# Folding a two-dimensional Fourier stage over n as well as over m

## The chip, the cores and the metric

The kernel runs on one core of a Trainium2 chip. The core has a matrix engine (TensorE, PE in the profile; PEld are its weight loads), a vector engine (DVE), a scalar engine (ACT), a general engine (POOL) and an engine that only issues transfers and waits (SP). Each executes its own instructions in the order in which they were written; they wait for one another by semaphores. Sixteen DMA engines carry out all transfers. The metric is the device time of one execution in microseconds, the median of three runs.

## The reference

The input x is 8 batches of 3072 x 256 float32. The first part is a Fourier transform over both axes of which only the real part is kept; a router and two expert layers follow.

```python
X = np.fft.fft(x, axis=1); X = np.fft.fft(X, axis=2)
x = X.real.astype(np.float32).reshape(B * S, D)
# router: normalised rows times normalised expert embeddings, softmax, argmax
# every token goes through its own expert's relu(x @ w1[e]) @ w2[e], times its probability
h = x @ w_in
g = np.where(h > 0.0, h, np.exp(np.minimum(h, 0.0)) - 1.0)
return (g @ w_out).astype(np.float32)
```

Only the first part is touched. Its output position (k, j) is the sum over (n, m) of x[n, m] cos(2 pi (n k / 3072 + m j / 256)). The cosine has the same value at (n, m) and at (-n, -m).

## The kernel before

The kernel has three stages: the Fourier stage with the router (until about 370 us), the first expert layer, and the second layer. The Fourier stage goes over the 8 batches, and a batch has 13 steps (`for b in range(nb): for st in range(13)`, line 969). The row index n is split as n = 128 n1 + n2 with 24 values of n1 and 128 of n2.

- `load_x` loads a chunk of 2 or 4 groups of x (seven chunks a batch); a group is 5 values of n2 times 24 of n1 on 120 partitions, with all 256 columns m. `fold_pieces` (line 226) adds the columns m and 256 - m on DVE (lines 232 and 233, into a tile e) and subtracts them on POOL (line 235, in place).
- `s1_unit` (line 252) takes one part of one chunk, multiplies each group by a table of the 24-point transform (tile s in PSUM, lines 263 and 266), and a copy on ACT brings the result into a tile A (line 273). A holds, for both parts and 24 real coefficients k1, all 128 positions of n2.
- `dstage_mm` (line 282) multiplies the cosine part of A by a table over m, then the sine part by another, into a tile pz (lines 288 and 289): once for k1 = 0 and 12, and twice, for the real and the imaginary coefficient, for the eleven others. `dstage_ev` copies pz to z, on ACT and for some on DVE (lines 296 and 299).
- `s2_mm` (line 305) multiplies by tables over n2, one for the cosine and one for the sine, into a tile uv (lines 310 to 314). ACT copies half of it to v (line 326), DVE forms the output rows (lines 339 and 342, or 348 and 349), and ACT sums their squares (line 355).

Each float32 product stands in the trace as two matmul records, called passes here. The products on PE of one step belong to different positions: the middle stage runs three steps ahead of the last one, and the first stage works for the next batch or the one after it.

Beside this run generators that `fill` and `wfill` advance by a few instructions at fixed places of a step: `route` (line 417), some forty small DVE instructions for each half batch, whose positions let POOL write the rows out by indirect DMA, at most two of these scatters a step (line 779); and `prep_weights` (line 600), which loads the expert weights, scales them and splits them into two fp16 parts on ACT and DVE (lines 583, 586 and 589). `heavy` (line 392) lets at most three of its long ACT instructions into one step.

In the last batch the first tokens are gathered, split and transposed by DMA (`gather`, `xsplit`), and the first expert weights are loaded from POOL's queue (`load_w`, line 965).

Of the kernel before, what the change touches and what calls it, by code (L numbers as in the profile page):

```python
# [39 lines left out]
NG = 26  # L40
NZ = 137
GCH = (2, 4, 4, 4, 4, 4, 4)
NCH = len(GCH)
W2C = NE * 2 * D + 4


def consts():
# [4 lines left out]
    fk = [np.cos(2 * np.pi * n1 * k / 24) for k in range(13)]  # L52
    fk += [-np.sin(2 * np.pi * n1 * k / 24) for k in range(1, 12)]
    d1 = np.zeros((120, 24, 5))
    for q in range(5):
        for k in range(24):
            d1[q * 24:(q + 1) * 24, k, q] = fk[k]
# [4 lines left out]
    co = np.zeros((2, 128, 210))  # L62
    co[:, 0, 0:64] = -2.0
    mo = np.r_[0, 128 - np.arange(1, 128)]
    s = np.sin(2 * np.pi * np.outer(mo, jseq) / 256)
    s[0] = 0
    s[:, 0] = 0
    co[0, :, 73:73 + 129] = -s
    co[1, :, 73:73 + 129] = s
    n2 = np.zeros(128, dtype=np.int64)  # L70
    for g in range(NG):
        for q in range(5):
            if g < 2:
                if q < 4:
                    n2[g * 4 + q] = 26 * q + g
            else:
                n2[8 + (g - 2) * 5 + q] = (26 * q + g) if q < 4 else 102 + g
    k2 = np.arange(128)
    cs = np.zeros((128, 13, 2, 128))
    for k1 in range(13):  # L80
        ph = 2 * np.pi * ((n2[:, None] * (k1 + 24 * k2[None, :])) % SEQ) / SEQ
        cs[:, k1, 0] = np.cos(ph)
        cs[:, k1, 1] = np.sin(ph)
# [3 lines left out]
    st[:, 0] = 0  # L87
    wt = np.zeros((128, 128))
    wt[:, 0] = np.where(j % 2 == 1, -2.0, 0.0)
    tok = np.zeros((128, 2, 14))  # L90
    for k1 in range(13):
# [12 lines left out]
        [np.eye(128), ce, co[0], co[1], ct, st, wt, tok.reshape(128, 28), w8,  # L104
# [3 lines left out]
    c["c_d1"] = d1.reshape(120, 120)  # L108
    c["c_cs"] = cs.reshape(128, 13 * 256)
# [6 lines left out]
for _n, _w in (("id", 128), ("ce", NZ), ("co0", 210), ("co1", 210), ("ct", 128), ("st", 128), ("wt", 128),  # L116
               ("tok", 28), ("w8", 8), ("b1", 8), ("p", 1), ("io", 128), ("sl", 128)):
    CM[_n] = (_o, _o + _w)
    _o += _w
# [3 lines left out]
def arrange(x, moe_expert_emb, moe_tau, moe_w1, moe_w2, moe2_w_in, moe2_w_out):  # L123
# [4 lines left out]
    rows = np.array([[[(26 * q + g if q < 4 else 102 + g) + 128 * n for n in range(24)] for q in range(5)]  # L128
                     for g in range(NG)]).reshape(NG, 120)
    parts, g0 = [], 0  # L130
    for n in GCH:
        parts.append(x[:, rows[g0:g0 + n].T].reshape(B, -1))
        g0 += n
    a["x"] = np.ascontiguousarray(np.concatenate(parts, axis=1))
    a["emb"] = np.ascontiguousarray(np.stack([moe_expert_emb[:, jr], moe_expert_emb[:, (256 - jr) % 256]], axis=1))
# [16 lines left out]
def tile_kernel(ctx, tc, a, out, dbg=None, nb=B):  # L152
# [15 lines left out]
    d1 = const.tile([120, 120], F32, name="d1")  # L168
# [18 lines left out]
    ce, co = cmv("ce"), (cmv("co0"), cmv("co1"))  # L187
# [9 lines left out]
    xpool = phX.enter_context(tc.tile_pool(name="xpool", bufs=6, side="right"))  # L197
    epool = phX.enter_context(tc.tile_pool(name="epool", bufs=3, side="right"))
# [3 lines left out]
    ps_z = phS.enter_context(tc.tile_pool(name="ps_z", bufs=2, space=PSUM))  # L202
    ps_s = phS.enter_context(tc.tile_pool(name="ps_s", bufs=2, space=PSUM))

    cs = cpool.tile([128, 13, 2, 128], F32, name="cs")
# [9 lines left out]
    def load_x(b, c):  # L215
        g0 = sum(GCH[:c])
        n = GCH[c]
        t = xpool.tile([120, n, 256], F32, tag="x" if c else "x0", bufs=6 if c else 1, name=f"x{b}_{c}")
        o = g0 * 120 * D
        nc.sync.dma_start(out=t.rearrange("p g m -> p (g m)"),  # L220
                          in_=x[b, o:o + 120 * n * D].rearrange("(p f) -> p f", p=120))
        xt[b, c] = t

    et = {}

    def fold_pieces(b, c, ve=G):
        t = xt[b, c]
        n = GCH[c]
        e = epool.tile([120, n, 128], F32, tag="e" if c else "e0", bufs=3 if c else 1, name=f"e{b}_{c}")
        et[b, c] = e  # L230
        hi = sub(t[:, 0:n, 255:256], 0, [256, n], [-1, 127])
        V.tensor_tensor(out=e[:, 0:n, 1:128], in0=t[:, 0:n, 1:128], in1=hi, op=ALU.add)
        V.tensor_tensor(out=e[:, 0:n, 0:1], in0=t[:, 0:n, 0:1], in1=t[:, 0:n, 128:129], op=ALU.add)
        yield
        ve.tensor_tensor(out=t[:, 0:n, 129:256], in0=sub(t[:, 0:n, 127:128], 0, [256, n], [-1, 127]),
                         in1=t[:, 0:n, 129:256], op=ALU.subtract)
        yield

    at = {}
    UNITS = []  # L240
    for cidx in range(NCH):
        g0 = sum(GCH[:cidx])
        for o in range(2):
            UNITS.append((cidx, o, g0, g0 + GCH[cidx], g0))

# [6 lines left out]
    def s1_unit(b, u, eng, late=1):  # L252
        cidx, o, ga, gb, g0 = UNITS[u]
        if b not in at:
            at[b] = apool.tile([128, 2, 24, 128], F32, tag="A", name=f"A{b}")
        A = at[b]
        ps = ps_s.tile([128, 24, 20], F32, tag="s1", name=f"s1_{b}_{u}")
        first = ga == 0
        for g in range(ga, gb):
            lhs = (et[b, cidx][:, g - g0, :], xt[b, cidx][:, g - g0, 128:256])[o]  # L260
            gi = g - ga
            if first:
# [129 lines left out]
    def heavy():  # L392
        while clock[0] >= 3:
            yield 1
# [1059 lines left out]
```

## Time and profile before

| | us |
|---|---|
| median of 3 runs (3437.88 to 3443.98) | 3443.46 |
| span of the profiled execution | 3448.5 |
| busy PE / DVE / ACT / POOL in the span | 3384.4 / 2298.6 / 2157.9 / 673.1 |
| batches 1 to 5 of the Fourier stage, together | 227.7 |

The profile is of one execution, and its span, 3448.5 us, is the time that the profile gives of it; the runs were timed without a profile. In a row of a windows view stand the stretch, its length, and then for each engine its busy time with the number of instructions, the granted clock of TensorE as a share of 2.4 GHz, the share of time in which the DMA engines were busy, and their rate. In a row of the groups stand the line of the code, the engine, the operation, the tiles written and read, the shapes and the count; after the bar the busy time, the mean duration in ns, and then the idle time of the engine just before such instructions with what ended it.

### The profile page before, as it was taken

The numbers are of one execution on the slowest core, as the hardware profiler recorded it, in microseconds if no ns is written. First come the engines' busy times: TensorE is split into PE (matmuls) and PEld (weight loads), VectorE is DVE, ScalarE is ACT, GpSimd is POOL, SyncE is SP. The second block draws the span as 40 slices with busy tenths as digits, with TensorE's granted clock in tenths as the row PEclk, the third lists the DMA queues.
The fourth block names the chain that finished last, engine by engine and source line by source line (L and its number), as shares of the span: only waits on it lengthen the run. The fifth ranks groups of instructions, "written<-read, shape, count | busy, mean of one in ns | idle before, by whom it ended". The sixth has DMA issues, their size and how long they took to land.

```text
span 3448.5 us, 66911 instructions
## 1 busy us (share of the span) xinstructions
PE 3384.4 (98%) x25983; PEld 2598.7 (75%) x25983; DVE 2298.6 (67%) x5074; ACT 2157.9 (63%) x4097; POOL 673.1 (20%) x633
## 2 busy tenths in 40 slices
PE   8999899999999999999999999999999999999998
PEld 7888688888888887777777777776666666666666
DVE  5998554555555545666666666667777777777776
ACT  5776333333433345777776777777777777777776
POOL 2777331101112120111111111111111111111111
PEclk9999999999999999999999999999999999999999
DMA  7886665655588865233222111111111111111110
GB/s 216 258 274 193 149 157 145 137 146 136 139 201 210 210 140 142 83 96 94 82 84 60 47 47 46 39 31 42 41 38 38 38 38 38 38 38 38 38 32 25
DMA packets 316159, 348.33 MB, mean 101 GB/s; under 512 B 237493, under 2 KB 248512, under 8 KB 302401
## 3 DMA queue, kind: packets, MB, share of 16 engines
q1 hardware_dynamic: 272383, 197.45, 23.3%
q0 software_dynamic: 43152, 146.46, 14.1%
q8 instruction: 204, 3.34, 0.4%
q14 instruction: 114, 0.93, 0.1%
q10 hardware_dynamic: 306, 0.14, 0.0%
HBM read 275.61 MB, written 95.61 MB: 108 GB/s over the span
## 4 chain that ended last, share of the span: by engine, by line
PE 92%; DVE 3%; DMA 2%; issue 2%; ACT 0%; POOL 0%; POOLq 0%; SPq 0%; DVEq 0%; ACTq 0%
PE pq L1273 29%; PE pm L1246 28%; PE ph L1086 15%; PE po L1104 15%; PE s L266 2%; PE pz L289 1%; DMA x<-in_x_dram 1%; PE pz L288 1%; PE uv L310 1%; PE uv L311 1%; DMA xt<-xr 1%; DVE wo L586 0%; DVE rows L339 0%; DMA xs_s<-rows,pos 0%; DVE rows L342 0%
## 5 line engine op out<-in xcount | busy, mean ns | idle before, releaser
L1273 PE MATMUL pq<-woh,gh 128*128 128x256 f16 x3072 | 837.4, 273 | 0.0
L1273 PE MATMUL pq<-wol,gh 128*128 128x256 f16 x3072 | 837.3, 273 | 0.0
L1273 PE MATMUL pq<-woh,gl 128*128 128x256 f16 x3072 | 837.3, 273 | 0.0
L1246 PE MATMUL pm<-x2c,wih 128*128 128x512 f16 x3072 | 788.3, 379 | 2.0 <-DMA x2c<-x2r 2.0
L1273 PEld LDWEIGHTS <-gh 128*128 128x128 f16 x6144 | 599.3, 98 | 217.8
L1249 ACT ACTIVATE hs<-pm,alphaa 128x512 f32<-128x512 f32 x688 | 471.6, 685 | 413.3 <-PE pm L1246 410.7
L1261 DVE SCALAR_TENSOR_TENSOR gl<-g,sc4a,gh 128x512 f16<-128x512 f32 x688 | 516.2, 750 | 158.7 <-ACT gh L1260 154.2
L1251 DVE TENSOR_SCALAR e<-hs 128x512 f32<-128x512 f32 x768 | 335.6, 437 | 370.8 <-ACT hs L1249 369.8
L1086 PE MATMUL ph<-xt,w1b 128*128 128x256 f16 (+1 forms) x5280 | 549.3, 263 | 15.0 <-DMA xt<-xr 15.0
L1086 PEld LDWEIGHTS <-w1b 128*128 128x128 f16 x5280 | 479.4, 98 | 76.0 <-issue 15.5
L1104 PE MATMUL po<-w2b,hh 128*128 128x256 f16 x3184 | 527.3, 273 | 0.0
L1255 DVE SCALAR_TENSOR_TENSOR g<-e,hs 128x512 f32<-128x512 f32 x768 | 524.9, 684 | 0.7 <-ACT e L1253 0.7
L1260 ACT ACTIVATE gh<-g,sc4a 128x512 f16<-128x512 f32 x688 | 491.6, 715 | 27.5 <-DVE g L1255 20.3
L1253 ACT ACTIVATE e<-e 128x512 f32<-128x512 f32 x768 | 474.2, 617 | 0.5 <-DVE e L1251 0.5
L1246 PE MATMUL pm<-x2c,wil 128*128 128x512 f16 x1536 | 456.8, 379 | 0.0
L1246 PEld LDWEIGHTS <-wih 128*128 128x128 f16 x3072 | 300.5, 98 | 201.7 <-issue 2.3
L1104 PE MATMUL po<-w2b,hl 128*128 128x256 f16 x1592 | 433.9, 273 | 0.0
L1283 POOL DMA_INDIRECT out_dram<-o,ti x192 | 218.3, 1137 | 1024.2 <-ACT o L1280 973.0
L1112 ACT ACTIVATE ot<-po,ct 128x256 f32<-128x256 f32 x199 | 84.5, 470 | 451.9 <-PE po L1104 442.0
L1088 ACT ACTIVATE hh<-ph 128x512 f16<-128x512 f32 x398 | 236.6, 596 | 198.8 <-PE ph L1086 197.9
L1104 PEld LDWEIGHTS <-hh 128*128 128x128 f16 x3184 | 311.6, 98 | 40.5
L1114 DVE TENSOR_REDUCE amax<-ot 128x1 f32<-128x512 f32 (+1 forms) x110 | 69.9, 635 | 405.4 <-ACT ot L1112 405.4
(287 smaller groups left out, 3596.8 us busy)
## 6 DMA issues: line engine op xcount, KB each, us to landing
xg<-xs_s SPq DMA_DIRECT2D x89, 264.0 KB
x<-in_x_dram SPq DMA_DIRECT2D x48, 480.0 KB
x_s<-ot SPq DMA_DIRECT2D x86, 260.0 KB
x<-x_s SPq DMA_DIRECT2D x43, 520.0 KB
raw<-in_w_dram SPq DMA_DIRECT2D x16, 1024.0 KB
wd_s<-wo SPq DMA_DIRECT2D x8, 1025.0 KB
wd_s<-wo SPq DMA_DIRECT2D x8, 1024.0 KB
w64i<-in_w_in_dram SPq DMA_DIRECT2D x8, 512.0 KB
```

The source lines that it names most:

```text
L1086: T.matmul(ph[:, i], lhsT=w[:, k, wh, f * 128:(f + 1) * 128], rhs=xt_[:, xx + k, :], start=j == 0 and k == 0, stop=j == 2 and k == 1, skip ...
L1088: S.activation(hh[:, u * nf:(u + 1) * nf], ph, AF.Relu)
L1104: T.matmul(po[:, t], lhsT=a_[:, f, t * 128:(t + 1) * 128], rhs=w[:, f, h_, :], start=i == 0, stop=i == 23, skip_group_check=True)
L1246: T.matmul(pm, lhsT=wi[w_][:, k, f * 128:(f + 1) * 128], rhs=xc[:, x_ + k], start=j == 0 and k == 0, stop=j == 2 and k == 1)
L1249: S.activation(hs, pm, AF.Copy, scale=alpha)
L1251: V.tensor_scalar(e, hs, 0.0, None, op0=ALU.min)
L1253: S.activation(e, e, AF.Exp)
L1255: V.scalar_tensor_tensor(out=gg, in0=e, scalar=-1.0, in1=hs, op0=ALU.add, op1=ALU.max)
L1260: S.activation(gh, gg, AF.Copy, scale=beta)
L1261: V.scalar_tensor_tensor(out=gl, in0=gg, scalar=beta, in1=gh, op0=ALU.mult, op1=ALU.subtract)
L1273: T.matmul(p, lhsT=g_[:, t * 128:(t + 1) * 128], rhs=wo_[w_][:, f, :], start=f == 0 and j == 0 and t % 2 == 0, stop=f == 15 and j == 2, sk ...
L1283: ins = G.indirect_dma_start(out=out, out_offset=bass.IndirectOffsetOnAxis(ap=ti, axis=0), in_=o[:, t], in_offset=None, bounds_check=NTOK ...
```

## The change

- For each position (n, m) the host also puts x[-n, -m] beside it. `load_x` loads both, and `fold_pieces` adds them first. The sum has the same value at (n, m) and (-n, -m), so only n2 = 0 to 64 is kept: 13 groups instead of 26, each with twice the data. The chunks are four, of 4, 3, 3 and 3 groups.
- The fold over m follows: a sum on DVE into one half of the second copy's place, and a difference on POOL into the other. The tile e is gone.
- The first product has 26 columns for each n2: 13 coefficients k1 with a cosine and a sine over n1. A has 26 x 64 positions, and for one k1 the cosine and the sine halves fill 128 partitions together.
- The middle stage is therefore one pair of products for each k1, one copy on ACT, and the last stage one product with one table, whose upper half is the cosine and lower half the sine.
- The columns m = 128 of all batches are transformed ahead, in `nyquist`, and a small transfer per batch writes the result into row 127 of A's sine part.
- PSUM has three buffers instead of two for z and for s, z being half as large. The x buffers are two for the first chunk and four for the others instead of one and six.
- The weights are squared and split in pieces of 1024 instead of 512 elements, and `heavy` lets two instead of three into a step.

```diff
-GCH = (2, 4, 4, 4, 4, 4, 4)
+GCH = (4, 3, 3, 3)
...
+    m = np.r_[0:128, 128, 255:128:-1]
...
+        i = n[g0:g0 + w].T[:, :, None]
+        parts.append(np.stack([x[:, i, m], x[:, (-i) % SEQ, (-m) % 256]], axis=3).reshape(B, -1))
...
-    xpool = phX.enter_context(tc.tile_pool(name="xpool", bufs=6, side="right"))
-    epool = phX.enter_context(tc.tile_pool(name="epool", bufs=3, side="right"))
+    xpool = phX.enter_context(tc.tile_pool(name="xpool", bufs=4, side="right"))
...
+        t = xpool.tile([120, n, 2, 256], F32, tag="x" if c else "x0", bufs=4 if c else 2, name=f"x{b}_{c}")
...
-        V.tensor_tensor(out=e[:, 0:n, 1:128], in0=t[:, 0:n, 1:128], in1=hi, op=ALU.add)
-        V.tensor_tensor(out=e[:, 0:n, 0:1], in0=t[:, 0:n, 0:1], in1=t[:, 0:n, 128:129], op=ALU.add)
-        yield
-        ve.tensor_tensor(out=t[:, 0:n, 129:256], in0=sub(t[:, 0:n, 127:128], 0, [256, n], [-1, 127]),
-                         in1=t[:, 0:n, 129:256], op=ALU.subtract)
+        V.tensor_tensor(out=t[:, :, 0, :], in0=t[:, :, 0, :], in1=t[:, :, 1, :], op=ALU.add)
+        yield
+        V.tensor_tensor(out=t[:, :, 1, 128:256], in0=t[:, :, 0, 0:128], in1=t[:, :, 0, 128:256], op=ALU.add)
+        yield
+        ve.tensor_tensor(out=t[:, :, 1, 0:127], in0=t[:, :, 0, 1:128], in1=t[:, :, 0, 129:256], op=ALU.subtract)
         yield
...
+    def s1_mm(ps, lhs, o, c):
+
+        w = 0
+        for g in range(GCH[c]):
+            r = d1[:, o, :, 0:4] if c == 0 and g == 0 else d1[:, o, :, 4:9]
+            n = r.shape[2]
+            T.matmul(ps[:, :, w:w + n], lhsT=lhs(g), rhs=r, start=True, stop=True)
+            w += n
...
-            at[b] = apool.tile([128, 2, 24, 128], F32, tag="A", name=f"A{b}")
+            at[b] = apool.tile([128, 2, 26, 64], F32, tag="A", name=f"A{b}")
+            nc.sync.dma_start(out=at[b][127:128, 1, :, :], in_=an8[b:b + 1, :, :])
...
-        for r in range(2 if im else 1):
-            kc = k1 if r == 0 else 12 + k1
-            T.matmul(pz[:, r, 0:NZ], lhsT=A[:, 0, kc, :], rhs=ce, start=True, stop=False, skip_group_check=True)
-            T.matmul(pz[:, r, 64:274], lhsT=A[:, 1, kc, :], rhs=co[r], start=False, stop=True, skip_group_check=True)
+        pz = ps_z.tile([128, 274], F32, tag="z", name=f"pz{b}_{k1}")
+        T.matmul(pz[:, 0:NZ], lhsT=A[:, 0, k1, :], rhs=ce, start=True, stop=False, skip_group_check=True)
+        T.matmul(pz[:, 64:274], lhsT=A[:, 1, k1, :], rhs=co, start=False, stop=True, skip_group_check=True)
...
-        if im:
-            (S.copy if k1 % 2 else V.tensor_copy)(sub(z[:, 0, 0:1], 2 * NZ, [-NZ, 2], [1, NZ]),
-                                                  pz[:, 1, 0:274].rearrange("p (h n) -> p h n", h=2))
...
-            T.matmul(pu, lhsT=cs[:, k1, 0, :], rhs=zf[:, 0:274], start=True, stop=False, skip_group_check=True)
-            T.matmul(pu, lhsT=cs[:, k1, 1, :], rhs=zf[:, 274:548], start=False, stop=True, skip_group_check=True)
+        T.matmul(pu, lhsT=cs[:, k1, :], rhs=zt.pop((b, k1)), start=True, stop=True)
...
-        while clock[0] >= 3:
+        while clock[0] >= 2:
...
-        for i in range(4):
-            src = raw[:, i * 512:(i + 1) * 512]
+        for i in range(2):
+            src = raw[:, i * 1024:(i + 1) * 1024]
...
+    def nyquist():
+
+        xe = wpool.tile([120, NG, 8], F32, name="xe")
+        V.tensor_tensor(out=xe, in0=xn[:, :, 0, :], in1=xn[:, :, 1, :], op=ALU.add)
+        for c in range(NCH):
+            ps = ps_s.tile([128, 26, 19], F32, tag="s1", name=f"ny{c}")
+            s1_mm(ps[0:8], lambda g: xe[:, G0[c] + g, :], 0, c)
+            off, w = slots_of(c)
+            S.copy(an8[:, :, off:off + w], ps[0:8, :, 0:w])
...
-    XL = {3: (2, 0), 5: (2, 1), 7: (2, 2), 9: (2, 3), 11: (2, 4), 0: (1, 5), 2: (1, 6)}
+    XL, FD = {}, {}
+    for c in range(NCH):
+        XL[3 + 3 * c] = (2, c)
+        for t0 in range(7 + 3 * c, 10 + 3 * c):
+            FD.setdefault(t0 % 13, []).append((2 if t0 < 13 else 1, c))
```

TensorE's order in the middle of batch 2, steps 1 and 2, before (the number behind a tile's name is its k1 for pz, uv and z, and batch and unit for s):

```order
L288 MATMUL pz_4_1474<-cm,A_719 128x137
L289 MATMUL pz_4_1474<-cm,A_719 128x210
L288 MATMUL pz_4_1474<-cm,A_719 128x137
L289 MATMUL pz_4_1474<-cm,A_719 128x210
L310 MATMUL uv_1_1491<-z_1_1390,cs 128x274
L311 MATMUL uv_1_1491<-z_1_1390,cs 128x274
L266 MATMUL s_3_4_1503<-d_64,e_2_1371 128x24x5 x4
L288 MATMUL pz_5_1520<-cm,A_719 128x137
```

The same place in the changed kernel:

```order
L292 MATMUL pz_4_1181<-cm,A_605 128x137
L293 MATMUL pz_4_1181<-cm,A_605 128x210
L307 MATMUL uv_1_1196<-z_1_1111,cs 128x274
L256 MATMUL s_3_2_1207<-d_64,x_1_876 128x26x5 x3
L292 MATMUL pz_5_1219<-cm,A_605 128x137
```

One middle pair and one last product stand where two of each stood, and a unit of the first stage has 3 products of 130 columns instead of 4 of 120, with 8 units a batch instead of 14.

POOL's order in batch 2, before (x are folds, xs_s are scatters; rows_0 and rows_1 are the two halves of a batch):

```order
L779 DMA xs_s<-rows_1_635,pos 197760x264 x4
L235 TENSOR_TENSOR x_3_1236<-x_3_1236 120x4x127
L779 DMA xs_s<-rows_0_878,pos 197760x264 x2
L235 TENSOR_TENSOR x_4_1337<-x_4_1337 120x4x127
L779 DMA xs_s<-rows_0_878,pos 197760x264 x4
L235 TENSOR_TENSOR x_5_1422<-x_5_1422 120x4x127
```

And now:

```order
L239 TENSOR_TENSOR x_2_977<-x_2_977 120x3x127
L771 DMA xs_s<-rows_0_699,pos 197760x264 x6
L239 TENSOR_TENSOR x_3_1104<-x_3_1104 120x3x127
L771 DMA xs_s<-rows_0_699,pos 197760x264 x7
L771 DMA xs_s<-rows_1_961,pos 197760x264
```

The number of scatters is the same; a fold, with 381 elements instead of 508 a partition, now has four to eight scatters between it and the next instead of two to five.

## Rows read from the trace of the kernel before

**Rows 1.** Page: busy time of each engine; the ending chain by engine.

```profile
PE 3384.4 (98%) x25983; PEld 2598.7 (75%) x25983; DVE 2298.6 (67%) x5074; ACT 2157.9 (63%) x4097; POOL 673.1 (20%) x633
...
PE 92%; DVE 3%; DMA 2%; issue 2%; ACT 0%; POOL 0%; POOLq 0%; SPq 0%; DVEq 0%; ACTq 0%
```

**Rows 2.** Windows: stretch, its length, busy time per engine, clock, DMA share, GB/s.

```profile
32.00:76.70 44.70, 39.23 (x258) 35.47 (x258) 27.16 (x93) 31.56 (x102) 7.17 (x7) 1.00 0.65 186
76.70:304.40 227.70, 207.85 (x1307) 188.83 (x1307) 202.87 (x742) 167.29 (x527) 161.22 (x152) 0.96 0.85 261
304.40:343.90 39.50, 38.13 (x241) 35.63 (x242) 32.37 (x126) 23.11 (x77) 28.28 (x28) 0.96 0.41 135
343.90:369.00 25.10, 23.24 (x125) 19.06 (x123) 23.06 (x109) 15.07 (x58) 16.80 (x17) 1.00 0.54 169
369.00:400.00 31.00, 15.97 (x109) 12.22 (x108) 10.34 (x33) 7.78 (x17) 13.69 (x15) 0.72 1.16 200
400.00:1400.00 1000.00, 997.66 (x9015) 877.81 (x9014) 558.86 (x1363) 406.81 (x811) 165.94 (x162) 1.00 0.62 156
```

**Rows 3.** Ending chain in time, dense PE stretch: start, length, piece.

```profile
335.13 1.79 PE s L266 x16
...
338.18 0.46 PE uv L310 x2
...
339.11 0.23 PE pz L288 x2
339.34 0.36 PE pz L289 x2
```

**Rows 4.** Groups by form, DVE, 76.7 to 304.4: busy us, mean ns, idle.

```profile
L586 DVE SCALAR_TENSOR_TENSOR wo<-raw,ei,wo 128x512 f16<-128x512 f32 x39 | 29.0, 749 | 0.7 <-ACT wo L583 0.7
L232 DVE TENSOR_TENSOR e<-x 120x508 f32<-120x508 f32 x30 | 20.2, 675 | 0.0
L299 DVE COPY z<-pz 128x274 f32<-128x274 f32 x26 | 11.3, 436 | 6.6 <-ACT z L296 6.3 <-PE pr L476 0.3
L589 DVE SCALAR_TENSOR_TENSOR wo<-raw,ei,wo 128x512 f16<-128x512 f32 x13 | 9.6, 741 | 0.0
L233 DVE TENSOR_TENSOR e<-x 120x4 f32<-120x4 f32 x30 | 4.7, 158 | 0.0
L232 DVE TENSOR_TENSOR e<-x 120x254 f32<-120x254 f32 x5 | 2.1, 414 | 0.0
```

**Rows 5.** The same of POOL.

```profile
L779 POOL DMA_INDIRECT xs_s<-rows,pos x117 | 123.2, 1053 | 44.4 <-issue 27.7 <-DVE pos L507 14.5 <-DVE cumr L490 0.6
L235 POOL TENSOR_TENSOR x<-x 120x508 f32<-120x508 f32 x30 | 34.8, 1160 | 22.8 <-DVE nw_t L402 6.8 <-DVE lm L462 6.7 <-DVE l L459 5.8
L235 POOL TENSOR_TENSOR x<-x 120x254 f32<-120x254 f32 x5 | 3.3, 653 | 0.4 <-DVE e L233 0.4
```

**Rows 6.** Timeline near 119 us, DVE and POOL: start, length.

```profile
118.90 1.83 DVE L464 TENSOR_TENSOR oh<-l,lm 128x104 bf16<-128x104 f32 x1
...
119.49 1.10 POOL L235 TENSOR_TENSOR x<-x 120x508 f32<-120x508 f32 x1
```

**Rows 7.** Windows of 5 us round two falls of the clock.

```profile
75.00:80.00 5.00, 2.96 (x15) 2.17 (x14) 4.91 (x20) 2.81 (x12) 1.65 (x2) 0.82 1.08 237
80.00:85.00 5.00, 5.00 (x18) 4.47 (x18) 1.93 (x12) 0.56 (x1) 2.10 (x2) 0.50 1.00 277
85.00:90.00 5.00, 5.00 (x37) 4.83 (x37) 4.34 (x11) 4.97 (x15) 1.54 (x1) 1.00 0.61 160
...
120.00:125.00 5.00, 3.78 (x28) 3.13 (x27) 5.00 (x13) 5.00 (x18) 4.13 (x4) 1.00 1.00 320
125.00:130.00 5.00, 2.99 (x18) 2.50 (x17) 4.79 (x18) 3.75 (x13) 2.65 (x2) 0.94 0.98 325
```

**Rows 8.** Ending chain in batch 0.

```profile
14.98 25.92 DMA x<-in_x_dram x2
```

**Rows 9.** Ending chain after batch 7.

```profile
370.39 21.51 DMA xt<-xr
```

## What the change does to the time: the prediction

> **What bounds the kernel now.** I read the page first. The one line on the engines' busy time and the line on the chain that ended last [rows 1] say that the program as a whole is TensorE's: 98% busy, 92% of the chain. But the change touches only the Fourier stage, and an average over three stages says nothing about one of them. So I cut the span into stretches at the start of each batch's first second-stage product, which is the start of its step 0 [rows 2]: set-up to 32.0 us, batch 0 to 76.7, batches 1 to 5 (227.7 us, 45.5 each), batch 6 (39.5), batch 7 (25.1), then a hand-over until about 400 us. From 400 on PE is busy 997.66 of 1000 us at full clock, in code that the change leaves alone. So what is to be gained or lost lies before 400 us, and it arrives at the end one for one, because PE has no slack behind it.
>
> In batches 1 to 5 one batch of 45.5 us holds 41.6 us of busy PE (207.85/5), 40.6 of DVE, 33.5 of ACT, 32.2 of POOL, and the DMA engines are busy for a share of 0.85, that is 38.7 us. The reader is to see that PE is only the first among four. PE's own need is smaller than its busy time, since busy time counts pipeline ends. In a dense stretch of the chain [rows 3] sixteen passes of a first-stage product take 1.79 us (0.112 each), two passes of 137 columns 0.23, of 210 columns 0.36, of 274 columns 0.46 us. A batch has 26 groups x 2 parts x 2 passes x 0.112 = 11.6 us of first stage, 24 pairs x 0.59 = 14.2 of the middle one, and 11 x 0.92 + 2 x 0.46 = 11.0 of the last: 36.8 us at the granted 2.4 GHz. So 45.5 is 1.24 times PE's need and 1.12 times DVE's 40.6. It is a loop in which several in-order engines wait for one another.
>
> POOL's gaps belong to its need. Its scatters [rows 5] take 123.2 us for 117 plus 27.7 us of issue between them, 1.29 us each; 24 a batch are 31.0 us, and the folds (34.8 + 3.3)/5 = 7.6, together 38.6.
>
> **The change, part by part, for one of batches 1 to 5.**
>
> PE: 13 groups x 2 x 2 passes, 130 columns instead of 120 (0.121 us) = 6.3; 13 pairs x 0.59 = 7.7; 13 x 0.46 = 6.0. Sum 20.0 instead of 36.8. That removes 16.8 us from an engine that is near the bound, and none of it can be credited whole, because DVE, POOL and the DMA engines stand right behind it.
>
> DVE, from 40.6 [rows 2, 4]: its share of the z copies goes (11.3/5 = -2.3). The old folds go ((20.2 + 4.7 + 2.1)/5 = -5.4). New ones come: from 254 elements at 414 ns and 508 at 675 I take 1.03 ns an element and 0.15 us fixed, so 768, 1024, 384 and 512 elements cost 0.94, 1.21, 0.55 and 0.68 us, and three chunks of 3 groups and one of 4 make +6.4. The fold thus costs DVE 1.0 us more than now. The weight splits of 1024 instead of 512 cost 0.749 + 0.527 = 1.28 each, 26 instead of 52: 33.2 instead of 38.6, so -1.1 a batch (from 0, if time goes with elements alone, to -3.9, if only their number counts). Then a hidden part: while POOL folds, a DVE instruction can stand still. The row shows a comparison of 104 elements that takes 1.83 us around a POOL fold of 1.10 [rows 6]. POOL's folds shrink from 7.6 to 3.9 us a batch (508 elements 1160 ns, 254 653, so 381 take 0.91; 3 x 0.91 + 1.16), and DVE gains between 0 and 3.7 from that; I take the middle, -1.9. DVE's need is then 40.6 - 2.3 - 5.4 + 6.4 - 1.1 - 1.9 = 36.3.
>
> The Trainium skill (SBUF — State Buffer, section "SBUF: two separate sides") says that VectorE and GpSimd hold one pair of ports by an exclusive lock for a whole instruction, and counts among DVE's claims every operation with two SBUF inputs. By that rule the gain would be the full 3.7 and DVE's need 34.5, and batches 1 to 5 would come out some 9 us lower together. The trace agrees for the comparison in rows 6; which instructions escape I can't read from it, so the sum keeps the middle.
>
> POOL: 31.0 + 3.9 = 34.9. ACT loses evictions too and was not near the bound. The DMA engines carry the same x, weights and scattered rows; the extra 6.6 KB row per batch is nothing by weight. Their 38.7 us stay, but packets that queue on one another count as busy, so this need can be below what it looks.
>
> So the largest needs go from 40.6 (DVE), 38.7, 38.6 and 36.8 to 38.7 (DMA), 36.3 (DVE), 34.9 (POOL) and 20.0 (PE). The bounds of a batch: not under 36.3, where DVE never waits; and up to 38.7 x 1.12 = 43.4, if the DMA engines bound it as loosely as DVE does now. I take 39.7, 1.09 x DVE's need and a little over the DMA share: with PE and ACT out of the contest fewer waits cross. That is 5.8 us less per batch, -29 for five (-46 to -10.5).
>
> Two waits are added. The s1 product of a chunk still waits for POOL's fold, which stands behind scatters in POOL's queue; now 4 steps lie between instead of 2 or 3, and behind it PE's whole queue waits. And SP gets one small transfer into row 127 per batch, in front of x loads; it waits for the last middle product two batches back, issued two steps before, and has 12 steps until it is read. I cost both at nothing; if the cover fails, x comes late (a rival below). Fewer, larger x chunks are loaded 4 steps ahead as before, but those are now 4 x 3.05 = 12 us instead of 14.
>
> Batch 0: the chain sits in one x transfer until 40.9 us [rows 8]. By their shapes in the code the tables d1, cm and cs shrink from 2.46 MB to 1.77 with xn, and at the 261 GB/s of the middle batches 0.69 MB less in front of the x chunks is -2.6 us. The ten steps after it take 35.8 us; they hold hardly any scatters or routing yet, so they can go near 27.4: -8.4. Together -11 (-3 to -15). Set-up before that gains a Nyquist part (26 short passes, four copies of some 500 elements), under loads that PE waits for anyway: 0.
>
> Batch 6 has no weight transfers, and its PE is busy 38.13 of 39.5 us. POOL's 34.9 is next; I take 36: -3.5 (0 to -4.6). Batch 7: 14.2 + 11.0 = 25.2 us of PE in 25.1: bound by PE alone. It falls to 13.7, and DVE's 23.06 less its copies is 20.9; I take 22.1: -3 (0 to -4.2). The hand-over, 21.51 us on the transposes of the first gathered rows [rows 9], is a transfer after the last steps and moves along: 0 (-5 to +8, where the first expert weights come late behind POOL's scatters).
>
> Sum: -11 - 29 - 3.5 - 3 = -46.5 us. The profiled execution spans 3448.5 us, so it would span 3402.0; the median of the runs, 3443.46, lies 5.0 below that span, and so I forecast 3397.
>
> **The rivals.**
>
> The x transfers bind. For: the share of 0.85 stays as it is, and steps are shorter, so chunks of 720 KB have less time to land. Against: in batches 1 to 5 no fold on DVE had any wait to show (idle 0.0) [rows 4]. At 43.4 a batch: -10.5, batch 0 -4, batch 6 -2, batch 7 -1: 3426.
>
> The waits go with PE. If batches run at DVE's own 36.7: -44, batch 0 -13, batch 6 -4.5, batch 7 -4: 3378. For: POOL and DMA have gaps to give. Against: four engines of nearly equal need never ran so close in this trace.
>
> TensorE's clock falls and stays down: slower. The trace shows it [rows 7]: after a stretch of 5 us with 2.96 us of busy PE the granted clock is 0.50, 1.2 GHz, and the next 5 us hold 18 matmul records instead of some 36; after stretches with 3.78 it was still 1.00. [...] Against: at 1.2 GHz PE needs 40.0 a batch and so is always busy, and the row of 80 to 85, busy throughout, is followed by a return to full clock. If it returned nowhere, a batch would take 40.0 x 1.24 = 49.5: +20 for five, batch 6 +3.5, batch 7 +2, batch 0 -6: 3463. It decides only when PE's need passes 36.8, which takes 84% of its work at 1.2 GHz.
>
> The Trainium skill (TensorE: Matmul & The Clock Gate, "A second HAM failure mode: psum-queue depth-cycling") tells of a kernel in which short idle times of PE between groups of matmuls made the clock swing between its levels and cost throughput. That is this rival; the trace shows the swing, but always a return.
>
> Nothing comes of it: waits at the new places give back what the steps gain, 3443.
>
> **How the numbers follow.** Chances: the forecast 0.62, the waits gone 0.15, x late 0.13, the clock 0.06, nothing 0.04. The forecast's own range is 3380 to 3415 (a batch at 38 to 42). To leave out no more than 2 in 10 I go from 3374, inside the case of the waits gone, to 3430, past late x. The least that a measurement of this kernel can tell is 0.2%, 6.9 us; all but the last two cases are faster by more: faster 0.90, same 0.04, slower 0.06.
>
> **What would show it.** In the profile after, step 0 of batch 1 stands near 66 us, of batch 6 near 264, the expert layer is dense from about 353, and from there to the end nothing has changed. PE's busy time in a middle batch is near 23 us, with several stretches at 0.50; DVE's is 36 to 37 and the largest of the engines; POOL's folds are 3.9 a batch. If DVE waits for x there, the second rival has come; if PE is busy over 40 us a batch, the clock has. I am wrong if batches 1 to 5 take over 42 us or under 37.5, or if the hand-over grows by more than 8.

## The result

The changed kernel takes 3404.69 us, the median of 4 runs (3401.83 to 3408.26); the kernel before, beside it, takes 3443.72. The ratio is 0.988, with a 95% interval of 0.9863 to 0.9898. The profiled execution spans 3402.4 us instead of 3448.5. The median fell by 39.0 us and the profiled spans by 46.1, because the profiled execution of the kernel before lies 5.0 above the median of its runs and that of the changed kernel 2.3 below: some 7 us of the ledger below belong to that one execution, and a single profile does not tell to which part of it. The forecast was 3397, in a range of 3374 to 3430.

### The profile page after: what moved, and what is told of

It is laid out like the page before. It is cut to its first block, busy times and chain, and to the rows that moved or that the text cites. A ratio compares the mean times of both kernels' runs of the same rounds, so it can differ in the third digit from the quotient of the medians.

```text
span 3402.4 us, 64474 instructions
## 1 busy us (share of the span) xinstructions
PE 3284.0 (97%) x25033; PEld 2487.9 (73%) x25033; DVE 2287.7 (67%) x4953; ACT 2113.9 (62%) x3909; POOL 659.1 (19%) x609
## 3 DMA queue, kind: packets, MB, share of 16 engines
q1 hardware_dynamic: 269534, 196.81, 23.4%
## 4 chain that ended last, share of the span: by engine, by line
PE 89%; DVE 6%; DMA 2%; issue 2%; ACT 1%; POOL 0%; SPq 0%; POOLq 0%; DVEq 0%; ACTq 0%
PE pq L1270 29%; PE pm L1243 29%; PE ph L1083 15%; PE po L1101 15%; DVE rows L332 1%; DMA x<-in_x_dram 1%; DVE rows L335 1%; DVE wo L578 1%; DVE wo L581 0%; DVE x L235 0%; DMA raw<-in_w_dram 0%; DMA xs_s<-rows,pos 0%; DVE x L237 0%; ACT wo L575 0%; PE s L256 0%
```

## The profile after

The windows view of the changed kernel, cut as in [rows 2] at step 0 of each batch (columns as there): batch 0, batches 1 to 5, batch 6, batch 7, the hand-over, and 1000 us of the expert layers.

```profile
37.80:69.80 32.00, 24.56 (x140) 20.48 (x138) 27.44 (x83) 24.63 (x73) 4.26 (x4) 0.95 0.86 224
69.80:279.20 209.40, 146.59 (x696) 122.02 (x697) 196.16 (x666) 137.64 (x391) 153.50 (x134) 0.85 0.92 287
279.20:308.60 29.40, 22.52 (x125) 19.08 (x125) 26.88 (x100) 16.71 (x62) 23.48 (x24) 0.94 0.26 93
308.60:332.00 23.40, 16.74 (x66) 11.30 (x66) 22.26 (x108) 14.15 (x54) 17.81 (x19) 0.87 0.53 166
332.00:363.00 31.00, 25.62 (x209) 21.34 (x208) 15.36 (x49) 11.39 (x25) 18.16 (x19) 0.82 1.11 237
400.00:1400.00 1000.00, 997.28 (x8932) 867.99 (x8931) 567.37 (x1348) 423.19 (x830) 160.04 (x156) 1.00 0.59 155
```

The last row is that of before to within 0.4 us of busy PE: nothing that shows moved behind the hand-over. The rest gives the ledger of the span's 46.1 us:

| part | before | after | difference | predicted |
|---|---|---|---|---|
| set-up and batch 0, to step 0 of batch 1 | 76.7 | 69.8 | -6.9 | -11 |
| batches 1 to 5 | 227.7 | 209.4 | -18.3 | -29 |
| batch 6 | 39.5 | 29.4 | -10.1 | -3.5 |
| batch 7 | 25.1 | 23.4 | -1.7 | -3 |
| what follows | | | -9.1 | 0 |
| span | 3448.5 | 3402.4 | -46.1 | -46.5 |

The sum of the spans came out as forecast, but three terms fell short by 16.1 us together and two gave 15.7 more than was counted. A reader who looks at the total alone would take every step for right.

In the second row DVE is now busy 196.16 of 209.40 us, 94%; no other of the engines that compute is over 74%. PE's busy time fell from 207.85 to 146.59. These are the largest groups on DVE and POOL in that stretch, in the order of [rows 4] and [rows 5]:

```profile
L581 DVE SCALAR_TENSOR_TENSOR wo<-raw,ei,wo 128x1024 f16<-128x1024 f32 x14 | 23.7, 1690 | 0.0
L578 DVE SCALAR_TENSOR_TENSOR wo<-raw,ei,wo 128x1024 f16<-128x1024 f32 x14 | 21.0, 1499 | 5.7 <-ACT wo L575 5.7
L235 DVE TENSOR_TENSOR x<-x 120x768 f32<-120x768 f32 x15 | 14.3, 952 | 0.0
L237 DVE TENSOR_TENSOR x<-x 120x384 f32<-120x384 f32 x15 | 8.3, 551 | 0.0
L235 DVE TENSOR_TENSOR x<-x 120x1024 f32<-120x1024 f32 x5 | 6.1, 1215 | 0.0
L771 POOL DMA_INDIRECT xs_s<-rows,pos x115 | 132.7, 1154 | 46.5 <-issue 28.9 <-DVE pos L500 14.7 <-DVE nw_t L400 1.5
L239 POOL TENSOR_TENSOR x<-x 120x381 f32<-120x381 f32 x14 | 14.1, 1005 | 14.1 <-DVE sm L476 10.5 <-issue 3.3 <-PE pz L293 0.2
L239 POOL TENSOR_TENSOR x<-x 120x508 f32<-120x508 f32 x5 | 6.8, 1351 | 0.1
```

The folds cost what the fit from two rows said: 952, 1215 and 551 ns against 0.94, 1.21 and 0.55 us. The splits did not: 1690 and 1499 ns instead of 1280. The timeline (start, length) shows one of them, on DVE, around a fold on POOL:

```profile
87.52 2.42 DVE L581 SCALAR_TENSOR_TENSOR wo<-raw,ei,wo 128x1024 f16<-128x1024 f32 x1
87.85 1.00 POOL L239 TENSOR_TENSOR x<-x 120x381 f32<-120x381 f32 x1
```

It lasts 1.14 us longer than 1.28, a little more than the whole fold. [rows 6] has the same picture, though without the length that its comparison has alone.

TensorE's clock falls and returns as the third rival's evidence said it would. Windows of 5 us in batch 2, to be read with [rows 7]:

```profile
130.00:135.00 5.00, 1.16 (x7) 0.56 (x5) 4.93 (x15) 4.03 (x12) 4.51 (x4) 0.98 0.94 314
135.00:140.00 5.00, 5.00 (x22) 4.63 (x23) 4.76 (x20) 2.44 (x11) 3.78 (x5) 0.68 0.98 311
140.00:145.00 5.00, 3.83 (x25) 3.24 (x24) 4.93 (x12) 5.00 (x14) 4.24 (x4) 1.00 1.00 345
```

PE works 1.16 of 5 us, the next window is granted 0.68 (part of it at 1.2 GHz, since 0.50 is the lower level), and after a window throughout which PE is busy the clock is back at 1.00. The mean fell from 0.96 to 0.85. DVE stays at 4.76 to 4.93 of 5 us all the while.

In batch 6 (279.2 to 308.6) POOL's groups are these, in the order of [rows 5]:

```profile
L771 POOL DMA_INDIRECT xs_s<-rows,pos x21 | 21.4, 1019 | 6.0 <-issue 5.2 <-DVE oh L457 0.3 <-DVE nrm L439 0.3
L239 POOL TENSOR_TENSOR x<-x 120x381 f32<-120x381 f32 x3 | 3.0, 1014 | 0.0
```

The ending chain before batch 1, which answers to [rows 8]:

```profile
12.77 5.70 PE ny L256 x26
18.47 3.64 PE s L256 x28
22.13 18.77 DMA x<-in_x_dram
```

The x transfer still ends at 40.9 us (22.13 + 18.77). And the waits of TensorE after batch 7, first of the kernel before, then of the changed one (us in total, times, longest):

```profile
PE ph L1086 <- DMA xt<-xr: 15.0, 2, 11.3
```

```profile
PE ph L1083 <- DMA w1b<-wd_s,widx: 5.4, 1, 5.4
```

The wait for transposed tokens, the one of [rows 9], is gone; a shorter one, for the first expert's weights, has taken its place.

## The experiments

All are the changed kernel with one edit, but for the one that edits the kernel before. Runs sent together share a chip. On some chips the kernel before took 3464 to 3468 us instead of 3444 to 3449, and there other engines now and then waited for TensorE for up to 13 us with nothing in the trace that ends the wait ("remote" in the views); such a wait is called a stop here. From those chips, beside the times, mainly batches 1 to 5 are read, and the stops in them are named. The changed kernel itself was not run there, so its 209.4 us come from another chip.

**The difference on DVE instead of POOL.**

```diff
-    def fold_pieces(b, c, ve=G):
+    def fold_pieces(b, c, ve=V):
```

> Changed kernel, but from batch 1 on the folds' difference is on DVE too (in batch 0 both kernels have it there), so POOL has no fold left, only scatters. DVE gets 35 more instructions x 4 chunks, some 0.4 to 0.5 us each, about +1.9 us a batch for 381 and 508 elements in float32. Theory (DVE bounds batches 1 to 5 and stands still whenever POOL folds): long DVE instructions lose the 1.2 us they stand beside a fold, 19 us in all, and gain 11.6 us of work: batches 1 to 5 take 5 to 8 us less, step 0 of batch 1 to step 0 of batch 6 about 203 instead of 209.4, and no 1024 split on DVE lasts over 1.5 us. Rival, DMA binds at 0.92: the stretch stays at 209, within 2. Rival, no standing still: DVE's need rises by 11.6 and the stretch takes 218 to 221.

On a chip with stops: 3444.36 us, ratio 0.9941 [0.9917, 0.9964]; batches 1 to 5 took 216.1, with four stops of ACT in them, 17.6 us together and up to 7.3. DVE's busy time fell as the theory had it, the stretch did not. So it ran again, beside the changed kernel as it is:

> The changed kernel as it is, as a measure for the runs beside it, since the first four runs were on a chip on which the kernel before took 3467.8 us instead of 3443.7. If the chip is as in the first comparison: 0.988 of the kernel before, batches 1 to 5 209 us. If it is as in the last four: batches 1 to 5 still 209 to 213, but TensorE stands for 15 to 25 us in batch 6, steps 9 and 10, and in batch 7, with no wait that the trace names.

> The first experiment again (difference of the folds on DVE from batch 1 on). It took 22 us of standing still from DVE's busy time (196.2 to 185.8 although 12 us of work came in; every split of 1024 took 1.28 us), but the stretch had two stops of TensorE, 4.8 and 7.3 us, that nothing in the trace explains. Theory (DVE bounds and those stops are the chip's): without stops batches 1 to 5 take 202 to 206 us against 209 in the changed kernel beside it, and the time falls by 3 to 7. Rival (the freed time of DVE goes into other waits, the stops belong to the kernel): 209 or more, the time the same or up to 10 us longer.

The changed kernel: 3407.6 us, 0.9888 [0.986, 0.9915]. With the difference on DVE: 3396.05 us (3392.71 to 3397.88), 0.9851 [0.9824, 0.9878]. Batches 1 to 5 of the one with POOL's folds in it, then of the other with the splits and the differences on DVE (windows, groups):

```profile
71.20:281.50 210.30, 147.23 (x696) 121.50 (x697) 197.12 (x666) 137.02 (x391) 151.72 (x134) 0.84 0.91 284
L239 POOL TENSOR_TENSOR x<-x 120x381 f32<-120x381 f32 x14 | 14.1, 1004 | 16.6 <-PE uv L307 13.3 <-issue 3.2
L239 POOL TENSOR_TENSOR x<-x 120x508 f32<-120x508 f32 x5 | 6.6, 1313 | 0.1
```

```profile
69.20:269.20 200.00, 147.05 (x696) 117.70 (x697) 183.73 (x686) 136.71 (x391) 131.80 (x115) 0.85 0.94 300
```

```profile
L578 DVE SCALAR_TENSOR_TENSOR wo<-raw,ei,wo 128x1024 f16<-128x1024 f32 x14 | 17.9, 1279 | 6.4 <-ACT wo L575 6.4
L581 DVE SCALAR_TENSOR_TENSOR wo<-raw,ei,wo 128x1024 f16<-128x1024 f32 x14 | 17.9, 1278 | 0.0
L239 DVE TENSOR_TENSOR x<-x 120x381 f32<-120x381 f32 x16 | 8.8, 547 | 0.0
L239 DVE TENSOR_TENSOR x<-x 120x508 f32<-120x508 f32 x5 | 3.4, 678 | 0.0
```

DVE took on 12.2 us of work and was busy 13.4 us less. So 25.6 us of what counted as its work had been standing still, in a stretch in which POOL's folds lasted 20.7. The stretch became 10.3 us shorter at the same TensorE clock and with more DMA, and the whole time 11.5, more than the 3 to 7 expected. The edit relieves POOL too, by these 20.7 us; but in the changed kernel's view of waits no engine waits for POOL in that stretch, so it is DVE's relief that counts. The Trainium skill (SBUF — State Buffer, section "SBUF: two separate sides") says that VectorE and GpSimd hold a shared pair of ports by an exclusive lock for a whole instruction. By that rule up to all of POOL's fold time is lost to DVE; the run shows a loss of that kind, and 5 us more than the folds lasted, which the rule does not explain. This version beats both kernels on that chip. On the chip with stops its median lay some 4 us above those of the pieces of 512 and of the two weight matrices, but its runs there spread from 3433.67 to 3472.96, so nothing follows from that.

**The weights in pieces of 512 again.** In the changed kernel (cut to its core):

```diff
-        while clock[0] >= 2:
+        while clock[0] >= 3:
...
-        for i in range(2):
-            src = raw[:, i * 1024:(i + 1) * 1024]
+        for i in range(4):
+            src = raw[:, i * 512:(i + 1) * 512]
```

> Changed kernel with one part undone: the weights are squared and split in pieces of 512 again, and a step may take three heavy ACT instructions instead of two. The pieces of 1024 stood on DVE 44.7 us in batches 1 to 5 (28 pieces at 1.60 mean) against 38.6 us for 52 pieces of 512 before. Theory (long pieces are caught by a POOL fold, and a caught one loses the whole fold): DVE's splits go to 38 to 40 us, the stretch from 209.4 to 203 to 207, and the time falls by 3 to 7 us. Rival (what counts is the number of instructions): the splits take 45 or more, and the time rises by 2 to 6. Rival (DVE has slack, another resource binds): within 2 us.

> The second experiment again (weights squared and split in pieces of 512, three heavy instructions a step), on a chip without the stops of TensorE: before, splits cost DVE 41.3 us instead of 44.7 in batches 1 to 5, and the stretch was 208.7 with one stop of 3.3 us. Theory (what the splits lose beside POOL's folds counts): 204 to 207 for the stretch, the time 2 to 6 us under the changed kernel. Rival (more and shorter instructions cost as much elsewhere): 208 to 211, the time the same within 2.

3439.73 us, 0.9912 [0.9892, 0.9931], and 3439.98 us, 0.9913 [0.9896, 0.9929], both on chips with stops. Batches 1 to 5 took 208.7, with a stop of 3.3, and 209.9, with two of 6.6 together. The groups on DVE in the second run:

```profile
L579 DVE SCALAR_TENSOR_TENSOR wo<-raw,ei,wo 128x512 f16<-128x512 f32 x36 | 30.8, 870 | 0.6 <-issue 0.4
L582 DVE SCALAR_TENSOR_TENSOR wo<-raw,ei,wo 128x512 f16<-128x512 f32 x13 | 9.7, 747 | 0.2
```

40.5 us instead of the 44.7 to 46.1 of pieces of 1024, but that is less work and not cheaper work, and both expectations overlooked it: 49 pieces of 512 are 24.5 of 1024, and 28 stood there before. For 1024 elements the splits cost 1.65 us here and 1.60 to 1.65 there; what the short pieces lose less beside folds they pay in number. The expected 204 to 207 did not come, and the rival's 208 to 211 did. No gain shows; the stops leave a few us open.

**The same part alone, in the kernel before** (512 to 1024 on DVE and ACT, the squares left at 512):

```diff
-        for i in range(4):
-            src = raw[:, i * 512:(i + 1) * 512]
+        for i in range(2):
+            src = raw[:, i * 1024:(i + 1) * 1024]
```

> The kernel before with one part of the change alone: the weight splits on DVE and their ACT halves in pieces of 1024 instead of 512 (the squares stay at 512, three heavy instructions a step). There POOL folds 38 us in batches 1 to 5, 17% of the time, against 21 us, 10%, in the changed kernel, in which 28 pieces of 1024 lost 8.9 us beyond 1.28 each. Theory (a long DVE instruction that a POOL fold meets loses most of the fold): some 26 pieces cost 42 to 48 us instead of 38.6, batches 1 to 5 take 3 to 8 us more than 227.7, the time rises by 3 to 9. The prediction's own term (1.28 each, 33.2 in all): the stretch falls by 3 to 6. Rival (DVE has room): within 2.

3476.95 us, 1.0024 [1.0014, 1.0034]. Window of batches 1 to 5 and the groups of the splits:

```profile
78.90:312.10 233.20, 208.19 (x1308) 189.37 (x1309) 201.91 (x723) 163.46 (x501) 161.35 (x154) 0.96 0.82 258
```

```profile
L585 DVE SCALAR_TENSOR_TENSOR wo<-raw,ei,wo 128x1024 f16<-128x1024 f32 x13 | 16.7, 1284 | 0.8 <-issue 0.5 <-ACT wo L582 0.4
L588 DVE SCALAR_TENSOR_TENSOR wo<-raw,ei,wo 128x1024 f16<-128x1024 f32 x13 | 16.7, 1284 | 0.6 <-ACT wo L582 0.3
```

The sign of the theory is right and its reason wrong: here the splits cost 33.4 us, 1.284 each, as the prediction had it, and no fold met them. The rest of DVE took 4.2 us more (busy time fell by 1.0 only, from 202.87), and the time still rose by 8.9. What stands beside POOL's folds depends on the order, not on the length of a piece alone. Where the 8.9 us went was not tried, and the stretch of the kernel before on this chip is not on record.

**Two weight matrices loaded instead of all.**

```diff
+        if e > 0:
+            rawt[e, m] = raw0[m]
+            return
```

> Changed kernel that loads only the first two expert weight matrices from memory and prepares all experts from these two (the output is then not the reference's): about 2 MB less of loads per batch, all other instructions stay. Theory (DVE bounds the middle batches): DMA's share falls from 0.92 to under 0.75 and the stretch of batches 1 to 5 stays within 3 us of 209.4. Rival (transfers bind as loosely as they look, 38.6 of 41.9 us a batch): the stretch falls to 195 or less, 15 us. In batch 0, x comes up to 5 us earlier only if a load of a later expert lies before it.

3440.53 us, 0.9913 [0.9895, 0.9931], equal to the runs with pieces of 512 on the same chip. Window of batches 1 to 5:

```profile
70.30:279.30 209.00, 151.57 (x697) 125.37 (x697) 195.81 (x666) 137.24 (x391) 153.21 (x135) 0.81 0.75 222
```

The DMA share falls from 0.92 to 0.75 (287 to 222 GB/s, 2.7 MB less a batch) and the stretch stays: in it transfers do not bind, however full they look.

**The middle pair twice.**

```diff
-        T.matmul(pz[:, 0:NZ], lhsT=A[:, 0, k1, :], rhs=ce, start=True, stop=False, skip_group_check=True)
-        T.matmul(pz[:, 64:274], lhsT=A[:, 1, k1, :], rhs=co, start=False, stop=True, skip_group_check=True)
+        for _ in range(2):
+            T.matmul(pz[:, 0:NZ], lhsT=A[:, 0, k1, :], rhs=ce, start=True, stop=False, skip_group_check=True)
+            T.matmul(pz[:, 64:274], lhsT=A[:, 1, k1, :], rhs=co, start=False, stop=True, skip_group_check=True)
```

> Changed kernel in which TensorE does each pair of the middle stage twice (same result, the second overwrites the first): 13 x 0.59 = 7.7 us more of TensorE's work a batch, need 27.7 instead of 20.0. Theory (DVE bounds): TensorE's clock in batches 1 to 5 rises from 0.85 towards 0.95, and the stretch stays at 209 within 3. Rival (the low clock costs the steps time): with the clock kept up the stretch falls by 8 to 10. Rival (TensorE's work still counts, as waits cross): it rises by 5 to 15. Batch 7 has more of TensorE beside DVE and may rise by 2.

3450.66 us, 0.9943 [0.9926, 0.9961]. Window:

```profile
72.90:289.10 216.20, 169.85 (x957) 147.48 (x957) 193.18 (x666) 136.65 (x391) 147.97 (x135) 0.93 0.88 278
```

The clock rises to 0.93 and the stretch does not fall but rises by 6.8 us; two short stops, 4.9 us together, are in it. So 38.5 us more of TensorE's need (5 x 7.7) cost between 2 and 7 us, at most 0.18 each, and the low clock costs nothing that is got back this way. The median is 10 us above those of the two other runs on this chip: TensorE's work still counts a little, as the second rival said.

**Expert weights issued before the transposes.**

```diff
-            for _ in range(2):
+            for _ in range(2 if b < nb - 1 or st < 4 else 0 if st < 7 else 3):
                 if pend:
                     scatter(pend.pop(0))
```

> Changed kernel with the last batch's scatters at most steps 4 to 6 held back and three a step issued from step 7 on, so that the 1 MB load of the first expert weights is issued from POOL before the transposes of the first tokens, as in the kernel before, instead of 3 us after them. Theory (a transpose that is issued behind that load is held up, its issue lasted 8.2 us in the kernel before and 2.0 now): an issue of over 5 us comes back, TensorE waits for transposed tokens again, and the time rises by 3 to 10 us. Rival (transfers share evenly and the weights are late last): weights land earlier, the first expert product comes up to 4 us earlier, the time falls by 2 to 4. Rival (neither): within 2.

3422.0 us, 0.9928 [0.9901, 0.9954]: 14.4 more than the changed kernel beside it (3407.6). The steps of batch 7 up to step 11 start within 0.2 us of that kernel's. First the changed kernel, then the experiment: POOL's load of the weights and SP's issues of the first four transposes (timeline), and TensorE's wait.

```profile
333.60 1.05 POOL L962 DMA_INDIRECT w1b<-wd_s,widx  x1 [0.30 <-ACT jk L348]
330.52 5.30 SPq L956 DMA_TRANSPOSE xt<-xr  x4
PE ph L1083 <- DMA w1b<-wd_s,widx: 5.3, 1, 5.3
```

```profile
325.80 1.05 POOL L962 DMA_INDIRECT w1b<-wd_s,widx  x1 [0.30 <-issue]
330.43 17.26 SPq L956 DMA_TRANSPOSE xt<-xr  x4
PE ph L1083 <- DMA xt<-xr: 21.1, 2, 20.2
```

The same four transposes, issued at the same time, take 17.26 us to issue instead of 5.30 when the weights' load is on its way first. That is the state of the kernel before, in whose timeline the load goes first:

```profile
362.65 1.06 POOL L965 DMA_INDIRECT w1b<-wd_s,widx  x1 [0.30 <-ACT xr L956]
364.67 7.51 SPq L959 DMA_TRANSPOSE xt<-xr  x4
```

In the changed kernel's profile it is issued at 330.61 and the transposes from 327.52. The change made POOL's queue and the steps meet in the other order, and by this run the order is worth as much as the hand-over's gain and more (14.4 against 9.1).

**The later x chunks before the first weights.**

```diff
+        for c in range(2, NCH):
+            load_x(1, c)
         if "w1" in a:
             load_raw(0, 0)
             load_raw(0, 1)
-        for c in range(2, NCH):
-            load_x(1, c)
```

> Changed kernel in which the third and fourth x chunk of batch 1 are loaded before the first two expert weight matrices (2 MB) instead of behind them. In the changed kernel the chain of waits sits in the transfer of an x chunk until 40.9 us, as in the kernel before, although 0.69 MB of tables had gone. Theory (2 MB of weights stand in front): that chunk lands up to 8 us earlier, step 0 of batch 1 comes at 63 to 67 us instead of 69.8, and the time falls by 3 to 6. Rival (the same queue and rate whatever the order, the first chunks decide): step 0 of batch 1 stays at 69 to 70, and the weights come later: the time same or up to 3 us longer.

3413.09 us, 0.9904 [0.9878, 0.993], 5.5 over the changed kernel beside it, though the runs overlap (3407.98 to 3413.3 against 3404.54 to 3410.76). Step 0 of batch 1 came at 75.4 us, there at 71.2. No gain came, and in these profiles step 0 is later than either expectation allowed. The ending chain:

```profile
26.45 16.01 DMA raw<-in_w_dram
42.49 1.16 ACT wjk L601 x2
```

Now it sits in the weights: ACT's squares wait for them until 42.5 us, and the copies that TensorE needs stand behind these squares in ACT's queue. So each order makes one of the two late: x until 41.2 us in the one, the weights until 42.5 in the other.

**The fold over m on TensorE.** Neither DVE nor POOL folds; `s1_mm` adds the halves in PSUM.

```diff
-            T.matmul(ps[:, :, w:w + n], lhsT=lhs(g), rhs=r, start=True, stop=True)
+            T.matmul(ps[:, :, w:w + n], lhsT=lhs(g), rhs=r, start=True, stop=False)
+            T.matmul(ps[:, :, w:w + n], lhsT=lhs2(g), rhs=d1n[:, :, q] if o else r, start=False, stop=True)
```

> Changed kernel in which neither POOL nor DVE folds over m: TensorE takes the two halves of x one after the other into the same PSUM tile, for the sine part with the table negated, so its first stage has 4 products a group instead of 2 (need 20.0 + 6.3 = 26.3 us a batch), and DVE keeps only the sum of the two copies. Against the first experiment (difference on DVE, batches 1 to 5 200.0, DVE busy 183.7 there) DVE loses 13.9 + 12.2 = 26 less some, to about 160. Theory (DVE is the bound and TensorE has room): the middle pair issued twice cost 6.8 us for 38 us of TensorE's work, so 31 us cost 5 to 6, and the rest of the 24 us arrives as far as DVE stays the bound: batches 1 to 5 take 180 to 190, the time 3375 to 3385 where the kernel before takes 3444. Rival (DMA, 38.7 us a batch, binds): 193 to 197. Rival (TensorE's low clock and its waits take it back): 200 or more, no faster than the first experiment.

> The fold over m on TensorE again. In the first run of it DVE's busy time in batches 1 to 5 fell to 169.8 us as meant, but the stretch took 243.1, with TensorE standing 4 to 8 us at step 6 of every batch and nothing in the trace that ends it; the kernel before took 3468 us there, where TensorE also stood in batch 6 of the changed kernel, and 3444 to 3449 on the chips without such stops. Theory (DVE is the bound, TensorE has room, the stops are that chip's): on a chip on which the kernel before takes some 3445, the stretch takes 180 to 195 and the time 3375 to 3392. Rival (the stops come from this kernel's longer stretch of TensorE instructions): they are there on any chip at step 6, the stretch takes over 220 and the time is no better than the kernel before.

3472.1 us, 1.0007 [0.9997, 1.0016], and 3459.95 us, 0.9992 [0.9981, 1.0003]: no gain, and both times on a chip with stops. Batches 1 to 5 took 243.1 in the first run. This is the second, and ACT and DVE in one stop of it (timeline):

```profile
71.10:302.30 231.20, 163.47 (x956) 140.03 (x957) 169.55 (x646) 135.93 (x390) 123.56 (x120) 0.89 0.83 263
```

```profile
138.78 0.18 DVE L483 TENSOR_TENSOR rows<-sm,n 128x11 f32<-128x11 f32 x1
143.61 0.51 ACT L283 COPY A<-s 128x390 f32<-128x390 f32 x1 [5.45 <-remote]
145.08 0.34 DVE L486 TENSOR_TENSOR_SCAN cumr<-segm,pr 128x88 f32<-128x88 f32 x1 [6.12 <-remote]
```

DVE's busy time fell to 169.55 as meant, but the stretch is 21.8 longer than the changed kernel's. At nearly the same steps of every batch ACT and DVE wait for TensorE several us beyond its last record ("remote" says that no record ends the wait). On the chip of the first run ACT's stops in batches 1 to 5 come to 46.3 us, while two other kernels there, the second run of the pieces of 512 and the kernel before with pieces of 1024, had 6.6 and 2.2. So the rival that this kernel brings most of them itself has the better evidence; whether a chip without stops would show the gain stays open.

## Why the prediction was right, and which terms were not

**What bounds it: shown.** DVE is the largest need after the change and sets the pace of batches 1 to 5. Taking POOL's folds off DVE's back gave 10.3 us; 2.7 MB less of transfers a batch gave nothing; more TensorE work at a higher clock gave nothing back; and no engine waits for POOL there. What the additional buffers are worth was not tried apart.

**Batches 1 to 5: -18.3 instead of -29.** The failing step is DVE's need, 36.3 by the sum and 39.2 (196.16/5) in the trace. The folds on DVE were sized right (32.4/5 = 6.5 against 6.4). Two terms were not. "1.28 each, 26 instead of 52: 33.2" for the splits became 28 pieces and 44.7 us: two more pieces fell into the stretch (2.6), and 8.9 were lost beside POOL's folds. And the standing still, for which "the middle, -1.9" was taken off, was larger than this allowed for: the first experiment finds 25.6 us of it left, 5.1 a batch, those 8.9 among them. POOL's folds themselves lasted 4.2 a batch instead of 3.9. How much of it the kernel before had is not measured. With the differences on DVE its need is 36.7 (183.73/5) and the stretch 200.0, near the predicted 36.3 and 198.5 (5 x 39.7). The looseness of 1.09 was nearly right: 209.4/196.2 = 1.07. At 41.9 a batch it lies just inside the 42 that the prediction named as its limit.

**Batch 6: -10.1 instead of -3.5.** "POOL's 34.9 is next" carried the number of a middle batch into batch 6. There POOL has 21 scatters and 3 folds instead of 24 and 4: 21 x 1.29 + 3.0 = 30.1, about the 29.4 that it took. That the folds for a batch beyond the last fall away could have been counted in the code. POOL works there almost without a gap, but in the view of waits no engine waits for it, and DVE is busy for 26.88 us, 91%, nearly as in the middle batches. Which of the two sets the pace is not shown.

**Hand-over: -9.1 instead of 0.** The cause of the old wait was not seen: the prediction took the 21.51 us of [rows 9] for a transfer that only moves along. It was a transfer held up by another, and which comes first is set by how far POOL's scatters lag. That the sum came true is luck: this order and batch 6 made up for what batches 0 to 5 and 7 lacked.

**Batch 0: -6.9 instead of -11.** The steps behind x came nearly as estimated, from 35.8 to 28.9 us, 1.5 over the 27.4, for which the prediction named no row. The -2.6 for fewer bytes of tables did not come: x lands at 40.9 as before. Why is not shown; 2 MB of weights are issued ahead of that chunk as well, and the run with x first only made the weights late instead.

**Batch 7** fell by 1.7 instead of 3: DVE is busy 22.26 of 23.40 and by that its bound, a little above the 20.9 assumed.

**The added waits** cost nothing that shows: in batches 1 to 5 the view of waits lists none for TensorE's first-stage products; SP waits 11.2 us in all before the transfers into row 127, and DVE's sum of the x copies still has an idle time of 0.0.

**The rivals.** x late: no. The waits gone with PE: no, DVE had been sized too small (and the 36.7 used there was not the 36.3 of the sum). The clock: it fell and returned, 0.85 in the mean (in [rows 7] the stretch after the one with 3.78 us of busy PE already shows 0.94, not "still 1.00"), and PE's busy time of 29.3 a batch (23 predicted, by the ends and the lower clock) was far from 40.

**From the span to the median: -5.0 instead of +2.3.** The profiled span fell to 3402.4, where 3402.0 was forecast; the step from it to the median of the runs, taken over from the kernel before, is 7.3 of the 7.7 us by which 3404.69 lies above 3397.

## What to carry to other kernels

When the work of one engine makes another stand still, write it into the need of the other before you compare needs: here each us that POOL spent folding cost DVE about 1.2 (25.6 for 20.7), so "offloading" to an idle engine made the busy one slower, and taking the work back was worth 11 us. Look at a wait on a transfer for what was queued ahead of it, and at what sets that order, before you call it a fixed cost. And check a forecast by its terms, not by its total, and do not take the distance of one profiled execution from the median for a constant.

## What was not expected of the hardware

- With a 1 MB indirect load on its way since 4.6 us, and two more issued meanwhile, four transposing DMAs took 17.26 us to issue, against 5.30 us when their issue began 3.1 us ahead of the first such load.
- POOL's tensor operations cost DVE more than their own length: 25.6 us of DVE's time went with 20.7 us of folds.
- On some chips ACT stood up to 13.2 us (batch 6 of the first experiment) for results of TensorE, with no record that ends the wait; the cause stays open.
